# A recurrent transformer segment loop on one core: a weight ring kept across turns, and memory rows joined to the next tokens

## The chip, the core and the metric

The kernel runs on one core of one Trainium2 chip. TensorE (PE) multiplies, with its weight loads on a queue of their own (PEld); VectorE (DVE), ScalarE (ACT) and GpSimd (POOL) do the rest, and SyncE (SP) issues most of the transfers (DMAs). The metric is the time of one execution on the device, in microseconds (us); lower is better. Comparisons are between medians of runs on one chip.

## What is computed

Two independent halves stand side by side in the output. Half A is a dilated sliding attention over 2048 tokens (32 heads of 20, a window of 8). Half B is a transformer layer with a memory that goes through the sequence segment by segment:

```python
mem = mem0                                     # 8 x 640
for s in range(n_seg):                         # 64 segments of 32 tokens
    h = concatenate([mem, x[:, 32*s:32*s+32]])           # 40 rows of 640
    q, k, v = (einsum('btd,dhe->bhte', h, W) for W in (Wq, Wk, Wv))   # 32 heads of 192
    scores = where(mask, q k^T * scale, -1e9)  # mask: key is memory, or key <= query
    o = softmax(scores) v
    o = einsum('bhte,hed->btd', o, Wo)
    mem = o[:, :8];  outs.append(o[:, 8:])
```

The four weights are 640 x 6144 numbers each in bf16, 31.5 MB together, more than the core's SBUF holds. Each segment needs all of them, and a segment can't start before the memory rows of the one before are there.

## The kernel before, in words

The weights are cut into 64 units of 128 x 1920 numbers (480 KB), four heads at a time of one type: (Q, r, j), (K, r, j), (V, r, j) for r and j from 0 to 3, and 16 units (O, ..) of the output projection. 44 units stay in SBUF (`resident`, tiles w_..), 20 (`streamed`) are loaded in every turn from copies in DRAM (`ws_scr`, named ws_.._65 to ws_.._84 in the order in which a turn uses them, nearly every third unit) into a ring of five slots, the tile pool `b_ring`; its tiles show in the trace as t. `get(u)` (L359 to 364) issues the load at the place in the program where the unit is first used.

The work is staged. First come resident units, the copies of the streamed ones and half A (`run_a`). Then a phase L computes Q, K and V of the last 8 tokens of all segments at once, since they depend on no memory and nothing of the next segment depends on them in its own projections: x is loaded in 16 blocks of 128 rows and turned on TensorE (L253), the last 8 tokens of each segment go to XL, the first 24 to a scratch `xt_scr`, and the results to `qk_scr` and `v_scr`. The remaining 18 resident units are loaded behind L. Then four loops of 16 turns run `segment(s)`, one turn for each segment, and a tail projects the output of the last 8 rows.

In a turn HT holds the 32 rows (8 of memory, 24 of tokens) turned, 128 x 5 x 32. `proj` (L378) multiplies them by four units at a time, in 20 matmuls on four quarters of the array; `qk` brings Q and K out, `turn` turns them (L401, L404), `scores` and a softmax follow for each of two halves t, `vproj` makes V. `turn_p(t)` (L458) turns the probabilities P and those of the left-over rows, PL, a single tile that the softmax of either half writes (L439). `pv(t)` makes OT (L493), and `oproj` (L507) adds the output projection into Y, 12 matmuls for each unit. At the end DVE casts Y to ybf (L545), transposes it in 32 x 32 blocks into yt (L547) and copies the 8 memory rows into HT (L548); the 24 token rows of the next segment were put there by GpSimd (`put_x`, L346) from xt. ACT's queue stores ol_scr and, in four DMAs, the token rows of ybf (L550).

PE and SP run in the order in which the code is written (`manual_schedule`); a scheduler orders the other engines. So SP issues a turn's small loads between the weight loads: `load_left` (qkl, L337) behind `turn(2)`, whose GpSimd copies (L395) read the old qkl; `load_x` (xt, L343) behind `put_x`; `load_vl` (vl, L340) behind `pv(1)`, which reads the old vl. Each waits until the old content is read, and SP takes nothing else meanwhile. L364 is the line of the weight loads.

Of the kernel before, what the change touches and what calls it, by code (L numbers as in the profile page):

```python
# [149 lines left out]
def part_b(ctx, tc, B_x, B_mem0, B_Wq, B_Wk, B_Wv, B_Wo, out, ident, run_a):  # L150
# [8 lines left out]

    nc = tc.nc  # L160
# [6 lines left out]
    x2 = B_x.rearrange("b s d -> (b s) d")  # L167
# [39 lines left out]
    xt_scr = dram.tile([n_seg + 2, 128, 5 * NX], BF16, name="xt_scr")  # L207
# [21 lines left out]
    with ExitStack() as c1:  # L229
# [16 lines left out]

        XL = lone.tile([128, 5, n_seg, NL], BF16)
        for i in range(S // 128):
            xb = lx.tile([128, Dm], BF16, tag="xb")
            nc.sync.dma_start(xb[:], x2[128 * i:128 * i + 128, :])  # L250
            pt = lps.tile([128, 5, 4, SEG], BF16, tag="ps")
            for dc in range(5):
                nc.tensor.transpose(pt[:, dc].rearrange("p a b -> p (a b)"), xb[:, 128 * dc:128 * dc + 128], ident)  # L253
            xt = lx.tile([128, 4, 5, NX], BF16, tag="xt")
            cps[i % 2](xt[:].rearrange("p s c n -> p c s n"), pt[:, :, :, 0:NX])
            cps[(i + 1) % 2](XL[:, :, 4 * i:4 * i + 4, :], pt[:, :, :, NX:SEG])
            nc.sync.dma_start(xt_scr[4 * i:4 * i + 4].rearrange("s p n -> p s n"),
                              xt[:].rearrange("p s c n -> p s (c n)"))
        for k in range(2):
            nc.sync.dma_start(xt_scr[n_seg + k], xt[:, k].rearrange("p c n -> p (c n)"))  # L260
# [35 lines left out]
    ring = lctx.enter_context(tc.tile_pool(name="b_ring", bufs=N_RING))  # L296
# [11 lines left out]
    for g in range(2):  # L308
        m = mask[64 * g:64 * g + 64, :]
        nc.gpsimd.affine_select(out=m[:, NL:L], in_=m[:, NL:L], compare_op=ALU.is_ge, fill=-1e9, base=-NL,  # L310
                                pattern=[[-1, L - NL]], channel_multiplier=1)
        nc.gpsimd.memset(mask[64 * g:64 * g + NL + M, :], 0.0)
        nc.gpsimd.affine_select(out=m[:, 0:NL], in_=m[:, 0:NL], compare_op=ALU.is_ge, fill=-1e9, base=0,
                                pattern=[[-1, NL]], channel_multiplier=1)
        nc.gpsimd.affine_select(out=m[:, 0:NL], in_=m[:, 0:NL], compare_op=ALU.is_ge, fill=-1e9, base=NL + M - 1,
                                pattern=[[0, NL]], channel_multiplier=-1)
# [10 lines left out]

    QTW = 24 * L
    PL = cst.tile([128, 4, 4, NL], BF16)
    nc.gpsimd.memset(PL[:], 0.0)  # L330
# [3 lines left out]
    xt = cst.tile([128, 5, NX], BF16)  # L334
# [7 lines left out]
    def load_x(s):  # L342
        nc.sync.dma_start(xt[:].rearrange("p c n -> p (c n)"), xt_scr[s])  # L343

    def put_x():
        nc.gpsimd.tensor_copy(HT[:, :, M:32], xt[:])  # L346

    xr = one.tile([M, Dm], BF16, tag="xr")
    nc.sync.dma_start(xr[:], mem2)
    pm = acc([128, 5, M], BF16)  # L350
    for dc in range(5):
        nc.tensor.transpose(pm[:, dc, :], xr[:, 128 * dc:128 * dc + 128], ident[0:M, 0:M])
    nc.vector.tensor_copy(HT[:, :, 0:M], pm[:])
    load_x(0)
    put_x()
    load_left(0)
    load_vl(0)
    load_x(1)

    def get(u):  # L360
        if u in res:
            return view(res[u][:], u)
        t = ring.tile([128, US], BF16, tag="ws")
        nc.sync.dma_start(t[:], ws_scr[u][:])  # L364
        return view(t[:], u)

    def segment(s):
# [5 lines left out]
        def proj(ty, r):  # L373
            ps = acc([128, 384], name="pj")
            ws = [get((ty, r, j)) for j in range(4)]
            for dc in range(5):
                for j in range(4):
                    nc.tensor.matmul(ps[32 * j:32 * j + 32, :], lhsT=HT[:, dc, :], rhs=ws[j][:, dc, :],  # L378
                                     start=(dc == 0), stop=(dc == 4), tile_position=(0, 32 * j))
            return ps  # L380
# [7 lines left out]
        def turn(r):  # L388
            t = r // 2
            if r % 2 == 0:  # L390
# [3 lines left out]
                for T_, ty in ((QT, Q), (KT, K)):  # L394
                    nc.gpsimd.tensor_copy(T_[:, 0:QTW].rearrange("p (c j l) -> p c j l", c=6, j=4)[:, :, :, 0:NL],  # L395
# [6 lines left out]
            for T_, ty in ((cur["QT"], Q), (cur["KT"], K)):  # L402
                dst = T_[:, 0:QTW].rearrange("p (c j l) -> p c j l", c=6, j=4)[:, 3 * (r % 2):3 * (r % 2) + 3, :, NL:L]
                (nc.scalar.copy if ty == Q else nc.vector.tensor_copy)(dst, tp[:, ty])  # L404

        def scores(t):
# [13 lines left out]
            for n, (_, lo, rr, j, e, cc, hi) in enumerate(pl):  # L420
# [17 lines left out]
            nc.vector.tensor_tensor(P[t][:], t1[:, :, NL:L], sm[:].unsqueeze(2).to_broadcast([128, 8, 32]), op=ALU.mult)  # L438
            nc.vector.tensor_tensor(PL[:, :, 2 * t:2 * t + 2, :].rearrange("p j r k -> p r j k"),  # L439
                                    t1[:, :, 0:NL].rearrange("p (r j) k -> p r j k", r=2),  # L440
# [12 lines left out]
        def turn_p(t):  # L453
# [4 lines left out]
            nc.tensor.transpose(ptp[:, 2].rearrange("p e q -> p (e q)"), PL[:].rearrange("p j r k -> p (j r k)"), ident)  # L458
# [3 lines left out]
            nc.vector.tensor_tensor(PTL[:], ptp[:, 2, :, 0:16].unsqueeze(2).to_broadcast([128, 2, 2, 16]),  # L462
# [3 lines left out]
        def pv(t):  # L466
# [11 lines left out]
            for e in range(2):  # L478
                for j in range(4):
                    nc.tensor.matmul(ots[j][:, :, e, 0:16], lhsT=vl[G[j], e, 0:128], rhs=PTL[G[j], e], start=False,  # L480
# [187 lines left out]
```

## Time and profile before

| | us |
|---|---|
| median of 3 runs (5035.1 to 5046.54) | 5036.02 |
| the profiled execution | 4988.09 |
| its span, first to last instruction | 4986.3 |
| PE busy in the span | 2792.9 (56%) |
| PEld busy | 1755.1 (35%) |
| DVE, ACT, POOL busy | 1045.2, 605.4, 188.9 |

The page lists, for each group of instructions, the busy time, the mean time of one in ns, and the idle time of the engine just ahead of them with what ended it. A row on waits gives the engine, the line, what ended the waiting, the sum in us, how often and the longest. A row of the timeline gives the start and the length in us, the engine (SPq is SP's queue), line, operation and tiles, and in brackets the idle time ahead and its end. A row of windows gives the length of a stretch, each engine's busy time with its number of instructions, the granted TensorE clock as a share of its full 2.4 GHz, the mean busy share of the 16 DMA engines, and GB/s.

### The profile page before, as it was taken

What the parts mean: (1) busy time and instruction counts of PE and PEld (TensorE: products, weight loads), DVE (VectorE), ACT (ScalarE), POOL (GpSimd) and SP (SyncE); (2) the same over time, 40 slices, a digit from 0 to 9 for tenths busy, and PEclk for the clock granted to TensorE, in tenths of its full rate; (3) what the DMA queues carried; (4) which work ended last, traced back from release to release, by engine and by line L of the source; (5) the groups of instructions that cost most, each with busy time, mean ns of one, the idle gap of its engine ahead of it and who ended that gap; (6) DMA issues with size and microseconds to landing.
All of it is one profiled execution on the core that took longest, in us unless ns stands there. A gap on an engine that the chain in (4) does not pass through costs nothing. (4 is left out here: it accounts for less than half of the span.)

```text
span 4986.3 us, 107002 instructions
## 1 busy us (share of the span) xinstructions
PE 2792.9 (56%) x42572; PEld 1755.1 (35%) x42597; DVE 1045.2 (21%) x2433; ACT 605.4 (12%) x1444; POOL 188.9 (4%) x638
## 2 busy tenths in 40 slices
PE   1768555555555555555555555555555555555556
PEld 0543333333333333333333333333333333333334
DVE  1652111211112111111211111211111121121111
ACT  1222111111111111111111010111110111111111
POOL 0100000000000000000000000000000000000000
PEclk9988866666666666565666666566666566666667
DMA  8764844444444444444444444444444444444444
GB/s 242 247 214 118 254 159 152 157 165 153 152 149 151 158 154 157 161 143 151 143 152 162 160 143 153 143 155 156 157 165 140 157 146 155 155 157 165 150 155 143
DMA packets 388638, 803.95 MB, mean 161 GB/s; under 512 B 81768, under 2 KB 215600, under 8 KB 388576
## 3 DMA queue, kind: packets, MB, share of 16 engines
q1 hardware_dynamic: 325712, 756.93, 44.1%
q10 hardware_dynamic: 56880, 19.50, 1.6%
q0 software_dynamic: 5984, 26.67, 1.5%
q8 instruction: 42, 0.69, 0.1%
q14 instruction: 20, 0.16, 0.0%
HBM read 762.32 MB, written 50.47 MB: 163 GB/s over the span
## 5 line engine op out<-in xcount | busy, mean ns | idle before, releaser
L378 PE MATMUL pj<-t,HT 128*32 128x384 bf16 x4800 | 1193.3, 459 | 795.4 <-DMA t<-ws_3_2_74 298.0
L378 PEld LDWEIGHTS <-HT 128*32 128x32 bf16 x15360 | 546.8, 120 | 1524.9 <-issue 1192.7
L507 PEld LDWEIGHTS <-OT 128*32 128x32 bf16 x12288 | 482.5, 126 | 700.7 <-issue 593.2
L507 PE MATMUL Y<-t,OT 128*32 128x160 bf16 x3840 | 205.4, 323 | 599.1 <-DMA t<-ws_1_0_80 307.2
L385 ACT CAST nat<-pj 128x384 bf16<-128x384 f32 x256 | 121.5, 475 | 1709.4 <-PE pj L378 973.6
L385 DVE CAST nat<-pj 128x384 bf16<-128x384 f32 x256 | 142.8, 558 | 871.6 <-PE pj L378 810.6
L378 PE MATMUL pj<-w_0_0_147,HT 128*32 128x384 bf16 x320 | 120.1, 499 | 222.7 <-DVE HT L548 174.6
L458 PE MATMUL ptp<-ident,PL 128*128 128x128 bf16 x128 | 38.5, 301 | 293.4 <-DVE PL L439 293.4
L404 DVE COPY KT<-tp 128x384 bf16<-128x384 bf16 x256 | 91.1, 356 | 499.8 <-ACT QT L404 499.8
L404 ACT COPY QT<-tp 128x384 bf16<-128x384 bf16 x256 | 123.2, 481 | 481.1 <-PE L378 481.1
L493 DVE CAST OT<-ot 128x240 bf16<-128x240 f32 x256 | 92.5, 403 | 385.6 <-PE Y L507 240.2
L401 PE MATMUL tp<-ident,nat 128*128 128x128 bf16 x1536 | 167.2, 260 | 0.1
L401 PEld LDWEIGHTS <-nat 128*128 128x128 bf16 x1536 | 111.7, 115 | 115.7 <-issue 113.9
L545 DVE CAST ybf<-Y 128x160 bf16<-128x160 f32 x64 | 20.8, 325 | 612.9 <-remote 603.6
L422 PE MATMUL S<-KT,QT 128*64 128x40 bf16 (+1 forms) x4096 | 139.4, 190 | 8.6 <-DVE KT L404 7.6
L493 ACT CAST OT<-ot 128x240 bf16<-128x240 f32 x256 | 79.4, 362 | 531.1 <-PE pj L378 280.1
L462 DVE TENSOR_TENSOR PTL<-ptp,bd 128x64 bf16<-128x64 bf16 x128 | 24.5, 192 | 554.6 <-ACT PT L460 554.6
L422 PEld LDWEIGHTS <-QT 128*64 128x64 bf16 (+1 forms) x4096 | 117.2, 112 | 66.5 <-issue 59.8
L494 POOL COPY olt<-OT 128x192 bf16<-128x192 bf16 x128 | 44.4, 347 | 2168.1 <-ACT OT L493 1427.0
L458 PEld LDWEIGHTS <-PL 128*128 128x128 bf16 x128 | 16.3, 128 | 304.5 <-DVE PL L439 304.5
L378 PE MATMUL pj<-w_0_0_4235,HT 128*32 128x384 bf16 x320 | 123.4, 520 | 0.0
L378 PE MATMUL pj<-w_1_2_161,HT 128*32 128x384 bf16 x320 | 122.2, 505 | 0.0
(442 smaller groups left out, 5951.7 us busy)
## 6 DMA issues: line engine op xcount, KB each, us to landing
t<-ws_1_0_80 SPq DMA_DIRECT2D x66, 480.0 KB, 5.1
t<-ws_0_2_81 SPq DMA_DIRECT2D x66, 480.0 KB, 7.0
t<-ws_2_0_82 SPq DMA_DIRECT2D x66, 480.0 KB, 3.6
t<-ws_3_1_83 SPq DMA_DIRECT2D x66, 480.0 KB, 4.6
t<-ws_2_3_84 SPq DMA_DIRECT2D x66, 480.0 KB, 5.6
t<-ws_0_1_65 SPq DMA_DIRECT2D x65, 480.0 KB, 5.3
t<-ws_1_0_67 SPq DMA_DIRECT2D x65, 480.0 KB
t<-ws_1_3_68 SPq DMA_DIRECT2D x65, 480.0 KB, 7.2
```

The lines of the kernel that those rows point to most:

```text
L378: nc.tensor.matmul(ps[32 * j:32 * j + 32, :], lhsT=HT[:, dc, :], rhs=ws[j][:, dc, :], start=(dc == 0), stop=(dc == 4), tile_position=(0, 3 ...
L385: (nc.scalar.copy if ty == Q else nc.vector.tensor_copy)(n_[:], ps[:])
L401: nc.tensor.transpose(tp[:, ty, c].rearrange("p j l -> p (j l)"), n_[:, 128 * c:128 * c + 128], ident)
L404: (nc.scalar.copy if ty == Q else nc.vector.tensor_copy)(dst, tp[:, ty])
L422: nc.tensor.matmul(Sps[64 * e:64 * e + 64, 4 * rr + j, :], lhsT=QT[lo:hi, o:o + 64], rhs=KT[lo:hi, o:o + L], start=(e not in seen), stop=( ...
L458: nc.tensor.transpose(ptp[:, 2].rearrange("p e q -> p (e q)"), PL[:].rearrange("p j r k -> p (j r k)"), ident)
L462: nc.vector.tensor_tensor(PTL[:], ptp[:, 2, :, 0:16].unsqueeze(2).to_broadcast([128, 2, 2, 16]), bd[:, 2 * t:2 * t + 2].unsqueeze(1).to_br ...
L493: (nc.scalar.copy, nc.vector.tensor_copy)[j % 2](OTs[t][:, j], ots[j][:])
L494: nc.gpsimd.tensor_copy(olt[:, t], OTs[t][:].rearrange("p j r x l -> p (j r x) l")[:, :, 0:NL])
L507: nc.tensor.matmul(Yb[0][32 * g:32 * g + 32], lhsT=OTs[t][:, j, rr, x, NL:L], rhs=w[:, x, :].rearrange("p (c g q) -> p c g q", c=5, g=4)[: ...
L545: nc.vector.tensor_copy(ybf[:], Yb[0][:])
```

## The change

The ring becomes five tiles of their own that live through all turns. `done(us)`, called behind the last use of a unit, issues the load of the unit that stands five places further on in the cycle of 20, into the slot that has just been used; the first five loads stand ahead of the loops, and the last units of a turn are followed by the first loads of the next. PL becomes two tiles, one for each half. The rows of a segment are held as 24 tokens first and 8 memory rows last, and column blocks of 160 stand on the four quarters of the partitions; the rows of the weights are permuted to suit, so a Q, K or V unit is loaded by five DMAs, each from four blocks of 32 rows. The tokens of the next segment come as `xz`, untransposed with zeros in the memory rows (a scratch that DMAs fill straight from x), and one DVE instruction adds them to the memory rows of Y (`rows` is 1 there and 0 in token rows); one transpose then writes all of HT. ACT casts Y to yo for one store, and both stores go out on SP's queue. The L phase loads only the last 8 tokens, in four blocks. The core of the diff:

```diff
@@ weights
-    wv_ = [w.rearrange("(dc p) h e -> p dc (h e)", p=128) for w in (B_Wq, B_Wk, B_Wv)]
+    wv_ = [w.rearrange("(g c q) h e -> c g q (h e)", g=4, c=5) for w in (B_Wq, B_Wk, B_Wv)]
...
-            eng.dma_start(v, wv_[ty][:, :, 1536 * j + 384 * r:1536 * j + 384 * r + 384])
+            for c in range(5):
+                eng.dma_start(v[:, c, :], wv_[ty][c, :, :, 1536 * j + 384 * r:1536 * j + 384 * r + 384])
@@ the L phase
+        for g in range(4):
+            nc.scalar.dma_start(xz_scr[0:n_seg, g, 0:NX, :], x3[:, 0:NX, 160 * g:160 * g + 160])
...
-        for i in range(S // 128):
+        for i in range(NLT // 128):
             xb = lx.tile([128, Dm], BF16, tag="xb")
-            nc.sync.dma_start(xb[:], x2[128 * i:128 * i + 128, :])
...
+            nc.sync.dma_start(xb[:], x3[16 * i:16 * i + 16, NX:SEG, :])
@@ the ring
-    ring = lctx.enter_context(tc.tile_pool(name="b_ring", bufs=N_RING))
+    ws_ring = [cst.tile([128, US], BF16, name=f"ring{k}") for k in range(N_RING)]
+    def load_ring(k):
+        nc.sync.dma_start(ws_ring[k % N_RING][:], ws_scr[streamed[k % N_STR]][:])
...
     def get(u):
-        if u in res:
-            return view(res[u][:], u)
-        t = ring.tile([128, US], BF16, tag="ws")
-        nc.sync.dma_start(t[:], ws_scr[u][:])
-        return view(t[:], u)
+        return view(res[u][:] if u in res else ws_ring[pos[u] % N_RING][:], u)
+
+    def done(us):
+        for u in us:
+            if u in pos:
+                load_ring(pos[u] + N_RING)
@@ softmax, turn_p
-            nc.vector.tensor_tensor(PL[:, :, 2 * t:2 * t + 2, :].rearrange("p j r k -> p r j k"),
+            nc.vector.tensor_tensor(PLs[t][:, :, 2 * t:2 * t + 2, :].rearrange("p j r k -> p r j k"),
@@ the turn
         turn(2)
-        load_left(s + 1)
         qk(K, 3)
         vproj(0)
         turn(3)
         vproj(1)
+        load_left(s + 1)
...
         vproj(3)
-        put_x()
-        load_x(s + 2)
         oproj(0, 0, 4)
         turn_p(1)
         oproj(0, 4, 6)
         pv(1)
+        oproj(0, 6, 8)
+        oproj(1, 0, 4)
         load_vl(s + 1)
-        oproj(0, 6, 8)
-        nc.scalar.dma_start(ol_scr[s], olt[:].rearrange("p t x l -> p (t x l)"))
-        oproj(1, 0, 8)
-        ybf = one.tile([128, 5, 32], BF16, tag="ybf")
-        nc.vector.tensor_copy(ybf[:], Yb[0][:])
-        yt = one.tile([128, 5, 32], BF16, tag="yt")
-        nc.vector.transpose(yt[:].rearrange("p c q -> p (c q)"), ybf[:].rearrange("p c q -> p (c q)"))
-        nc.vector.tensor_copy(HT[:, :, 0:M], yt[:, :, 0:M])
-        for g in range(4):
-            nc.scalar.dma_start(out3[s][:, :, g, :], ybf[32 * g + M:32 * g + 32])
+        oproj(1, 4, 8)
+        nc.sync.dma_start(ol_scr[s], olt[:].rearrange("p t x l -> p (t x l)"))
+        z = one.tile([128, 160], BF16, tag="z", name="z")
+        nc.vector.scalar_tensor_tensor(out=z[:], in0=Yb[0][:], scalar=rows[:], in1=xz[:], op0=ALU.mult, op1=ALU.add)
+        nc.vector.transpose(HT[:].rearrange("p c t -> p (c t)"), z[:])
+        load_x(s + 2)
+        yo = one.tile([128, 160], BF16, tag="yo", name="yo")
+        nc.scalar.copy(yo[:], Yb[0][:])
+        nc.sync.dma_start(out3[s], yo[:])
```

The order of SP's queue from the first output-projection loads to the next turn, before (t is the ring's tile of the moment, ws_.. the copies in DRAM):

```order
L343 ISA
L343 DMA xt<-xt_scr 128x120
L364 ISA
L364 DMA t<-ws_1_0_80 128x1920
L364 ISA
L364 DMA t<-ws_0_2_81 128x1920
L340 ISA
L340 DMA vl<-v_scr 128x384
L364 REGISTER_ALU
L364 DMA t<-ws_2_0_82 128x1920
```

Here each small load stands right ahead of the weights that are used next. SP's queue at the end of a turn, after (ring_4485 to ring_4489 are the five slots):

```order
L355 ISA
L355 DMA ring_4488<-ws_1_3_68 128x1920
L349 ISA
L349 DMA vl<-v_scr 128x384
L355 ISA
L355 DMA ring_4489<-ws_1_2_69 128x1920
L553 ISA
L553 DMA ol_scr<-olt 128x384
L352 ISA
L352 DMA xz<-xz_scr 128x160
L561 ISA
L561 DMA out_dram<-yo 4x32x160
```

What moved: the weights around vl now belong to the next turn, and ol_scr, xz and the output store stand last, ahead of the next turn's first load, ws_2_1_70.

DVE at the end of a turn, before (Y is the output projection's sum, ybf and yt are its cast and its transpose):

```order
L545 REGISTER_ALU
L545 CAST ybf<-Y 128x160
L547 REGISTER_ALU
L547 STREAM_TRANSPOSE yt<-ybf 128x160
L548 REGISTER_ALU
L548 COPY HT<-yt 128x5x8
```

Cast, transpose and copy of the memory rows stand in a row. The same place after:

```order
L504 REGISTER_ALU
L504 CAST OT<-ot 128x240
L556 REGISTER_ALU
L556 SCALAR_TENSOR_TENSOR z<-Y,rows,xz 128x160
L557 REGISTER_ALU
L557 STREAM_TRANSPOSE HT<-z 128x160
```

Three instructions became two, and the transpose writes HT itself.

## Rows read from the trace of the kernel before

**Rows 1.** The page's costliest groups: the matmuls on ring tiles.

```profile
L378 PE MATMUL pj<-t,HT 128*32 128x384 bf16 x4800 | 1193.3, 459 | 795.4 <-DMA t<-ws_3_2_74 298.0
...
L507 PE MATMUL Y<-t,OT 128*32 128x160 bf16 x3840 | 205.4, 323 | 599.1 <-DMA t<-ws_1_0_80 307.2
```

**Rows 2.** Windows: start, prologue stretches, loop, and single microseconds at either clock.

```profile
0.00:50.00 50.00, 0.00 (x0) 0.00 (x0) 0.97 (x4) 1.28 (x1) 1.34 (x7) 1.00 1.00 286
...
610.00:4913.00 4303.00, 2369.83 (x39808) 1507.79 (x39808) 819.26 (x2112) 464.31 (x1152) 157.03 (x576) 0.62 0.44 154
...
2035.00:2036.00 1.00, 1.00 (x16) 0.47 (x12) 0.36 (x1) 0.46 (x1) 0.00 (x0) 0.50 0.96 277
2038.00:2039.00 1.00, 1.00 (x25) 0.45 (x22) 0.00 (x1) 0.86 (x2) 0.00 (x0) 1.00 0.12 46
...
360.00:390.00 30.00, 10.25 (x81) 6.85 (x81) 5.49 (x18) 6.82 (x16) 1.97 (x11) 0.58 0.66 145
390.00:600.00 210.00, 164.09 (x795) 79.36 (x804) 57.86 (x129) 50.41 (x128) 0.00 (x0) 0.90 0.57 174
```

**Rows 3.** Waits of TensorE for tiles other than ring tiles.

```profile
PE ptp L458 <- DVE PL L439: 293.4, 64, 4.8
...
PE pj L378 <- DVE HT L548: 174.6, 60, 5.1
...
PE pT L58 <- DMA xb<-in_A_x_dram: 89.2, 1, 89.2
```

**Rows 4.** Waits of SP's queue.

```profile
SPq L343 <- POOL HT L346: 1050.0, 64, 18.0
SPq L364 <- DMA out_dram<-ybf: 888.9, 240, 10.4
SPq L340 <- PE Y L507: 621.6, 64, 10.2
SPq L337 <- POOL KT L395: 478.7, 64, 8.6
```

**Rows 5.** The timeline of one turn, from 2020.90 to the next turn's start.

```profile
2021.43 0.32 SPq L364 DMA_DIRECT2D t<-ws_0_1_65  x1
...
2024.76 0.48 PE L378 MATMUL pj<-t,HT 128*32 128x384 bf16 x1 [3.38 <-DMA t<-ws_0_1_65]
...
2066.13 0.34 SPq L343 DMA_DIRECT2D xt<-xt_scr  x1
2066.68 0.32 SPq L364 DMA_DIRECT2D t<-ws_1_0_80  x1
...
2070.26 0.59 PE L507 MATMUL Y<-t,OT 128*32 128x160 bf16 x12 [4.92 <-DMA t<-ws_1_0_80]
...
2077.14 0.62 ACT L493 CAST OT<-ot 128x240 bf16<-128x240 f32 x2 [3.98 <-PE Y L507]
...
2077.64 0.36 SPq L364 DMA_DIRECT2D t<-ws_2_0_82  x1
...
2081.45 0.59 PE L507 MATMUL Y<-t,OT 128*32 128x160 bf16 x12 [4.43 <-DMA t<-ws_2_0_82]
...
2087.47 0.33 DVE L545 CAST ybf<-Y 128x160 bf16<-128x160 f32 x1 [9.61 <-remote]
...
2087.83 0.34 DVE L547 STREAM_TRANSPOSE yt<-ybf 128x160 bf16<-128x160 bf16 x1
2088.28 0.17 DVE L548 COPY HT<-yt 128x40 bf16<-128x40 bf16 x1
...
2088.71 0.48 PE L378 MATMUL pj<-w_0_0_147,HT 128*32 128x384 bf16 x1 [2.91 <-DVE HT L548]
```

**Rows 6.** The timeline: two successive steps of a projection, at either clock.

```profile
2035.36 0.53 PE L378 MATMUL pj<-w_1_0_163,HT 128*32 128x384 bf16 x1
...
2035.68 0.53 PE L378 MATMUL pj<-w_1_0_163,HT 128*32 128x384 bf16 x1
...
2038.07 0.34 PE L378 MATMUL pj<-t,HT 128*32 128x384 bf16 x1
...
2038.24 0.33 PE L378 MATMUL pj<-t,HT 128*32 128x384 bf16 x1
```

More of the change, by code (lines that the diff above doesn't have):

```diff
@@ L326, in part_b @@
     nc.vector.tensor_copy(bd[:], bdf[:].unsqueeze(2).to_broadcast([128, 4, 16]))
+    rows = cst.tile([128, 1], FP32)
+    nc.vector.tensor_copy(rows[:], bdf[:, 3:4])
     QTW = 24 * L
-    PL = cst.tile([128, 4, 4, NL], BF16)
-    nc.gpsimd.memset(PL[:], 0.0)
+    PLs = [cst.tile([128, 4, 4, NL], BF16, name=f"PL{t}") for t in range(2)]
+    for t in range(2):
+        nc.gpsimd.memset(PLs[t][:], 0.0)
     HT = cst.tile([128, 5, 32], BF16)
@@ L342, in load_x @@
     def load_x(s):
[L343 to L354, printed above, removed]
-    put_x()
+        nc.sync.dma_start(xz[:], xz_scr[s].rearrange("g t n -> (g t) n"))
+    def load_ring(k):
+        nc.sync.dma_start(ws_ring[k % N_RING][:], ws_scr[streamed[k % N_STR]][:])
+    z0 = one.tile([128, 160], BF16, tag="z")
+    nc.sync.dma_start(z0[:], xz_scr[0].rearrange("g t n -> (g t) n"))
+    for g in range(4):
+        nc.sync.dma_start(z0[32 * g + NX:32 * g + 32, :], mem2[:, 160 * g:160 * g + 160])
+    nc.vector.transpose(HT[:].rearrange("p c t -> p (c t)"), z0[:])
     load_left(0)
@@ L358, in part_b @@
     load_x(1)
+    for k in range(N_RING):
+        load_ring(k)
+    pos = {u: k for k, u in enumerate(streamed)}
     def get(u):
-        if u in res:
-            return view(res[u][:], u)
-        t = ring.tile([128, US], BF16, tag="ws")
-        nc.sync.dma_start(t[:], ws_scr[u][:])
-        return view(t[:], u)
+        return view(res[u][:] if u in res else ws_ring[pos[u] % N_RING][:], u)
[3 more added lines that the diff above has]
+                load_ring(pos[u] + N_RING)
     def segment(s):
@@ L379, in proj @@
                                      start=(dc == 0), stop=(dc == 4), tile_position=(0, 32 * j))
+            done([(ty, r, j) for j in range(4)])
             return ps
@@ L479, in pv @@
                 for j in range(4):
-                    nc.tensor.matmul(ots[j][:, :, e, 0:16], lhsT=vl[G[j], e, 0:128], rhs=PTL[G[j], e], start=False,
+                    nc.tensor.matmul(ots[j][:, :, e, NX:L], lhsT=vl[G[j], e, 0:128], rhs=PTL[G[j], e], start=False,
                                      stop=False, tile_position=(32 * j, 0), skip_group_check=True)
@@ L489, in pv @@
                 for j in range(4):
[L490 removed]
+                    nc.tensor.matmul(ots[j][64 * e:64 * e + 64, :, 2, NX:L], lhsT=vl[G[j], e, 128:192], rhs=PTL[G[j], e],
                                      start=False, stop=(e == 1), tile_position=(32 * j, 64 * e), skip_group_check=True)
@@ L506, in oproj @@
                     for g in range(4):
-                        nc.tensor.matmul(Yb[0][32 * g:32 * g + 32],
-                                         lhsT=OTs[t][:, j, rr, x, NL:L],
-                                         rhs=w[:, x, :].rearrange("p (c g q) -> p c g q", c=5, g=4)[:, :, g, :],
+                        nc.tensor.matmul(Yb[0][32 * g:32 * g + 32], lhsT=OTs[t][:, j, rr, x, 0:32],
+                                         rhs=w[:, x, 160 * g:160 * g + 160],
                                          start=(t == 0 and n == 0 and x == 0), stop=(t == 1 and n == 7 and x == 2),
                                          tile_position=(0, 32 * g))
+                done([(O, 2 * t + rr, j)])
         qk(Q, 0)
```

60 lines of the change are left out of this document (30 added, 30 removed).

## The prediction, made before the changed kernel had run

> **What bounds the kernel now.** I began with the costliest groups of the page and with what ended the idle time before each. TensorE has the most busy time, yet two of its rows have more idle time behind them than anything else in the loop: the matmuls on weights out of the ring (named t) waited 795.4 us in the projections and 599.1 us in the output projection, each time for a DMA [rows 1]. That is 1394.5 us, or 21.8 us of each of the 64 turns. The loop takes 4303 us, 67.2 us a turn, and in it the DMA engines are busy 0.44 of the time [rows 2], so it isn't the amount that is loaded that sets the time, but when the loads start.
>
> The waits of TensorE's other inputs come next: 293.4 us for PL, 4.6 us a turn, and 174.6 us for HT, 2.7 us a turn [rows 3]. Then I asked SP, which issues the loads in a fixed order, what it waits for: 1050.0 us for GpSimd's copy into HT ahead of the xt load, 888.9 us for landings of the out stores ahead of weight loads, 621.6 us for TensorE ahead of the vl load, 478.7 us for GpSimd's KT ahead of the qkl load [rows 4]. None of these is a wait for a free slot. A small load that must wait stands in the queue, and the weight loads behind it stand too.
>
> One turn shows it. Weight 80 is issued at 2066.68, right behind the xt load of 2066.13, and TensorE gets it at 2070.26 after 4.92 us of idleness; 82 is issued at 2077.64 and awaited until 2081.45, 4.43 us; at the turn's start 65 is issued at 2021.43 and awaited until 2024.76, 3.38 us [rows 5]. So a lone load takes 3.3 to 3.8 us from issue to matmul, and TensorE pays nearly all of it, since each is issued when TensorE is about to need it.
>
> Last I asked what is left of a turn when nothing waits. The loop has 39808 matmuls and as many weight loads on TensorE [rows 2], 1244 instructions a turn. From 2070.26 to the cast of OT at 2077.14, which needs the last of them, TensorE does five weight units of the output projection (24 instructions each), 6 for one turn of P and 96 for pv, 222 in all, in 6.88 us: 31.0 ns each. From 2081.45 to the ybf cast at 2087.47 it does eight units, 192, in 6.02 us: 31.4 ns [rows 5]. Neither stretch has a wait, both hold other shapes, and the pace is the same. I take 31 ns as the least that an instruction costs here over a long stretch, whatever its size: 1244 x 31 ns = 38.6 us. Projections are slower than that at the low clock: their steps come every 0.32 us there (five steps, 1.6 us for 40 instructions) and every 0.17 us at the high one [rows 6], at granted clocks of 0.50 and 1.00 [rows 2], that is 1.2 and 2.4 GHz. At 31 ns the 40 cost 1.24 us, so a projection at the low clock costs 0.36 us more, twelve of them 4.3 us.
>
> **The change part by part.** *The ring.* A load goes out when the unit five places ahead has been used, across turns too. Twelve projections use 15 of the 20 streamed units, so the lead of five units is four projections, at least 4 x 1.24 = 5.0 us of TensorE, against 3.3 to 3.8 us for a load; in the output projection a unit comes every 24 x 31 ns = 0.74 us and every third or fourth is streamed, so the lead is some 12 us. The 21.8 us go. What this costs: the 20 loads, 9.8 MB, must fit in the turn. At the loop's 154 GB/s over a share of 0.44 [rows 2], full engines would move 350 GB/s, so 9.8 MB and some 0.5 MB of small ones need 29 us of a turn. Busy share 0.69 of 42.6 us; it fits, unevenly.
>
> *SP's order.* The qkl load moves behind vproj(1), four steps later than turn(2), where its last reader is queued; vl behind four units of the last output half; xz to the end. The waits of [rows 4] that were for GpSimd or for DVE-fed work no longer stand before a weight that is needed soon. What is new on SP is the end of the turn: ol_scr, xz and out stand there, and out waits for ACT's copy of Y, which exists only when all of the turn's matmuls are done. Queued behind it is load 70, for the slot that unit 65 leaves, used in qk(Q,2). Moreover the program hands its DMAs eight completion semaphores in turn, and by that count 70 has that of the out store, so it waits for its landing, as SP does now for out stores [rows 4], 888.9 us over 240 waits, 3.7 us each. The store goes out about 1 us behind the last cast and lands some 3 us later; 70 wants to be issued about 1.5 us into the turn and used 5 us later. Bounds 0 and 2 us a turn; I take 0.8.
>
> *PL in two tiles.* turn_p(0) no longer reads what softmax(1) writes. The 4.6 us of PL go; the second half's stands before turn_p(1), behind vproj(2), pv(0), vproj(3) and four units, over 5 us of TensorE. Cost nothing, and if that cover failed, at most the old 4.6.
>
> *The turn's end.* Cast 0.33, transpose 0.34, copy 0.17 on DVE and the gaps take from 2087.47 to 2088.71, 1.24 us [rows 5]. The scalar_tensor_tensor that replaces the cast reads the same 128x160 from the same place; the trace has no row of it: between the cast's 0.33 and twice that; I take 0.33, since the size and the source are the same. The copy goes with its gap, about 0.28. So 1.0 us remains, 1.3 at the upper bound. ACT's copy yo is off this path; the new 40 KB store takes the place of four.
>
> Sum of a turn: 38.6 + 2.2 (half of the twelve projections at the low clock; all would be 4.3, none 0) + 1.0 + 0.8 = **42.6 us**. From above: 67.2 - 21.8 - 4.6 = 40.8, less 0.28, plus 0.8 = 41.3. I keep the first, as waits that now let a backlog drain will be gone. Loop: 64 x (67.2 - 42.6) = -1574 us.
>
> *The prologue.* Its weight loads take another form: five DMAs per unit, and each names on the source side four blocks of 32 rows where it named 128 rows. 66 units of 0.49 MB are so loaded: 30 ahead of part A's first x, 18 within the L phase, 18 ahead of the loop. In the first 50 us all 16 engines are busy at a share of 1.00 and move 286 GB/s [rows 2], 17.9 each. No row shows how a transfer of four blocks is dealt out. If over all 16, nothing changes. If by block over four, they move 71.5 GB/s together, a unit takes 6.9 us instead of 1.7, and the 32.4 MB take 453 us instead of 113. If on one engine, 1812 us. I take four: it is the only count that the new form has and the old hadn't. The Trainium skill states it so: "DMA: Bandwidth & Descriptors", section "Why a DMA increments its semaphore by 16 and not by 1", has a transfer use the largest number up to 16 that divides the first dimension of both sides, always the lowest-numbered engines; by that rule it is four, the same four each time, and no run here shows it. On four engines the 30 units take 206 us instead of 52, and part A waits for its x behind them, now 89.2 us [rows 3]: +155. L has 210 us [rows 2], and its 18 units (124 us instead of 31) lie largely beside its matmuls: +10, at most +93. The 18 ahead of the loop stand alone: +93 at most; the first turn uses them one after another, so I take +85. The 16 blocks that build XL, 30 us [rows 2], become four: -23. Sum **+227 us**, between -23 (16 engines) and +318.
>
> Against the profiled execution: 4988.1 - 1574 + 227 = 3641. The median of the runs stands 1.0096 above the profiled time (5036.02 over 4988.09), which gives 3676; I say **3675**.
>
> **The rivals.** (1) *The weights still go over 16 engines.* For it: they do so now; against it: the four blocks. 4988.1 - 1574 - 23 = 3391, times 1.0096: 3424.
>
> (2) *The ring becomes the bound.* In the projections the lead is four projections, and if loads that are queued behind one another take longer than that, each late slot delays the next. For it: at 2035 the DMA engines are at a share of 0.96 while TensorE works [rows 2]. Against it: over a turn 29 us of 42.6. Twelve stalls of 0.4 us, or a 4.5 us stall behind load 70: turn 47.1, loop -1286, 4988.1 - 1286 + 227 = 3929, times 1.0096: 3967.
>
> (3) *The clock stays high.* If no projection falls to 1.2 GHz and 70 isn't late, the turn is 38.6 + 1.0 = 39.6: -1766, 3449, times 1.0096: 3482. The loop's granted clock is now 0.62 [rows 2] with 27 us of waiting a turn, most of which goes. The Trainium skill says so of it ("TensorE: Matmul & The Clock Gate", "Part 1: The HAM clock gate"): the clock follows how busy the array has been. Against it: from 2035 TensorE is busy throughout, and the clock is 0.50 [rows 2]. Here the trace speaks for half and half.
>
> (4) *Slower: the weights go on a single engine.* If the new form puts each transfer on one engine, 32.4 MB at 17.9 GB/s are 1812 us, 1699 more than now; it decides from the point where the prologue grows by more than the loop gives back, 1574. 4988.1 - 1574 + 1699 - 23 = 5090, times 1.0096: 5139. Against it: the source has four blocks, and both sides would have to be dealt out by less than that.
>
> (5) *The change doesn't do what it says.* If SP is held at the out store as long as it now is held at xt and vl, the loads stay late and only PL and the copy are gained, 4.9 us a turn: 4988.1 - 314 + 227 = 4901, times 1.0096: 4948. Against it: only one of 20 loads stands directly behind that store with the slot free.
>
> **How the numbers follow.** Chances: forecast 0.62, (1) 0.12, (2) 0.13, (3) 0.08, (4) 0.02, (5) 0.03. The forecast's own range is turns of 41 to 45 us with a prologue of +150 to +318, 3500 to 3910. The range reaches down over (1) and (3) and leaves out (2), (4) and (5), 0.18: 3410 to 3930. A measurement of this kernel tells differences of about 0.3% from none; all cases but (4) are faster by more than that, with a little left for a tie: faster 0.97, same 0.01, slower 0.02.
>
> **What would show it.** Right: TensorE's rows on ring tiles lose their DMA waits; no wait for PL; the wait for HT stays at 2 to 3 us a turn; SP waits for TensorE alone, and for the out store at most once a turn; a turn is 41 to 45 us, the loop's DMA share 0.65 to 0.75; the first 50 us show 70 to 100 GB/s at a share near 0.3, and part A waits for x 200 to 250 us. Wrong: 286 GB/s at the start (rival 1); DMA waits on ring tiles in the Q and K projections (rival 2); a granted clock over 0.9 (rival 3). A turn under 38.6 us would fell the 31 ns.

## The result and the profile after

The median fell from 5035.56 to **3523.33 us** (four runs each, 3521.12 to 3534.18 after); the ratio is 0.700, with a 95% interval of 0.698 to 0.702. The prediction said 3675, with a range of 3410 to 3930. The profiled execution took 3534.18 us with a span of 3532.4.

Windows of the changed kernel: its first 50 us, and its loop, from the first projection to the last output projection.

```profile
0.00:50.00 50.00, 0.00 (x0) 0.00 (x0) 0.97 (x4) 0.00 (x0) 1.34 (x7) 1.00 0.65 152
...
833.50:3455.00 2621.50, 2125.61 (x39808) 1584.13 (x39808) 779.49 (x2046) 483.32 (x1215) 138.59 (x512) 0.88 0.75 252
```

The loop answers to the row of 4303 us in [rows 2]: 2621.5 us, 41.0 us a turn in place of 67.2, with the same number of TensorE instructions, at a granted clock of 0.88 where it was 0.62. (The row of 4303 us runs some 6 us past the last output projection; to the same point as here it was 67.1.) But the loop starts at 833.5 us and not at 610: the prologue grew by 223 us. The first 50 us move 152 GB/s at a share of 0.65, not the 70 to 100 at 0.3 that the prediction named as a sign; from 60 to 200 us it is 110 at 0.35. The first resident units are of the output projection, whose loads kept their form.

The page's costliest groups: two of the five ring slots.

```profile
L388 PE MATMUL pj<-ring_4488,HT 128*32 128x384 bf16 x960 | 223.4, 371 | 51.7 <-DMA ring_4488<-ws_3_3_73 43.9
...
L388 PE MATMUL pj<-ring_4485,HT 128*32 128x384 bf16 x960 | 206.4, 349 | 48.5 <-DMA ring_4485<-ws_2_1_70 43.9
```

They answer to [rows 1]: the ring tiles of the projections once had 795.4 us of idleness ahead of them; now the two worst slots have 100 and all five 144. In the output projection 599.1 us became 31.0, and these are for OT, not for a load (the row on Y below). What is left is late landings of 73 and, as foreseen, of 70, the load that stands behind the output store: 0.7 us a turn each. TensorE's waits in the loop and the first waits of SP:

```profile
PE pj L388 <- DVE HT L557: 156.5, 60, 2.6
...
PE ot L486 <- ACT PT L471: 68.1, 115, 0.7
...
PE Y L518 <- ACT OT L504: 31.0, 64, 0.5
...
SPq L355 <- PE L518: 782.1, 251, 5.6
SPq L355 <- PE pj L388: 287.7, 259, 7.0
```

No wait for PL is among them, HT's is 2.4 us a turn, and SP's largest waits are now for TensorE to be done with a slot; none of its rows names GpSimd [rows 4]. The turn's end, in the timeline:

```profile
2063.22 0.38 DVE L556 SCALAR_TENSOR_TENSOR z<-Y,rows,xz 128x160 bf16<-128x160 f32 x1 [6.60 <-issue]
...
2063.64 0.35 DVE L557 STREAM_TRANSPOSE HT<-z 128x160 bf16<-128x160 bf16 x1
...
2064.08 0.32 PE L388 MATMUL pj<-w_0_0_147,HT 128*32 128x384 bf16 x1 [2.61 <-DVE HT L557]
```

From the first DVE instruction to TensorE it takes 0.86 us, where it took 1.24 [rows 5].

### The profile page after: what moved, and what is told of

It reads as the page before. It is cut to its first block, busy times and chain, and to the rows that moved or that the text cites. A ratio compares the mean times of both kernels' runs of the same rounds, so it can differ in the third digit from the quotient of the medians.

```text
span 3532.4 us, 106126 instructions
## 1 busy us (share of the span) xinstructions
PE 2561.1 (73%) x42567; PEld 1831.5 (52%) x42592; DVE 1002.5 (28%) x2357; ACT 618.7 (18%) x1494; POOL 170.1 (5%) x572
## 5 line engine op out<-in xcount | busy, mean ns | idle before, releaser
L388 PEld LDWEIGHTS <-HT 128*32 128x32 bf16 x15360 | 479.4, 104 | 701.4 <-issue 204.5
L518 PEld LDWEIGHTS <-OT 128*32 128x32 bf16 x12288 | 614.3, 102 | 113.1 <-ACT OT L504 102.9
L388 PE MATMUL pj<-w_0_0_147,HT 128*32 128x384 bf16 x320 | 75.3, 373 | 278.4 <-DVE HT L557 156.5
L388 PE MATMUL pj<-ring_4488,HT 128*32 128x384 bf16 x960 | 223.4, 371 | 51.7 <-DMA ring_4488<-ws_3_3_73 43.9
L388 PE MATMUL pj<-ring_4487,HT 128*32 128x384 bf16 x960 | 236.8, 371 | 22.4 <-PE S L433 13.7
L388 PE MATMUL pj<-ring_4485,HT 128*32 128x384 bf16 x960 | 206.4, 349 | 48.5 <-DMA ring_4485<-ws_2_1_70 43.9
L388 PE MATMUL pj<-ring_4489,HT 128*32 128x384 bf16 x960 | 240.4, 381 | 0.2 <-DMA ring_4489<-ws_3_2_74 0.2
L388 PE MATMUL pj<-ring_4486,HT 128*32 128x384 bf16 x960 | 220.2, 367 | 21.0 <-DMA ring_4486<-ws_2_0_71 16.6
L412 PE MATMUL tp<-ident,nat 128*128 128x128 bf16 x1536 | 154.8, 234 | 27.5 <-DVE nat L396 26.9
L412 PEld LDWEIGHTS <-nat 128*128 128x128 bf16 x1536 | 95.0, 103 | 134.3 <-issue 90.3
L58 PE MATMUL pT<-ident,xb 128*128 128x128 bf16 x80 | 8.3, 241 | 215.5 <-DMA xb<-in_A_x_dram 212.5
L556 DVE SCALAR_TENSOR_TENSOR z<-Y,rows,xz 128x160 bf16<-128x160 f32 x64 | 24.6, 384 | 422.1 <-issue 422.1
L496 PE MATMUL ot<-PT,Vn 32*64 32x40 bf16 x2048 | 123.6, 182 | 0.0
L486 PE MATMUL ot<-PT,Vn 32*128 32x40 bf16 x2048 | 71.8, 178 | 68.5 <-ACT PT L471 68.1
```

What stands on the lines that cost most here:

```text
L58: nc.tensor.transpose(pT[:, c, :], xb[:, c * 128:(c + 1) * 128], ident)
L412: nc.tensor.transpose(tp[:, ty, c].rearrange("p j l -> p (j l)"), n_[:, 128 * c:128 * c + 128], ident)
L486: nc.tensor.matmul(ots[j][:, rr, e, :], lhsT=Vn[G[j], 2 * t + rr, e, 0:128], rhs=PT[G[j], rr, e, :], start=(rr == 0 and e == 0), stop=Fals ...
L496: nc.tensor.matmul(ots[j][64 * e:64 * e + 64, rr, 2, :], lhsT=Vn[G[j], 2 * t + rr, e, 128:192], rhs=PT[G[j], rr, e, :], start=False, stop= ...
L518: nc.tensor.matmul(Yb[0][32 * g:32 * g + 32], lhsT=OTs[t][:, j, rr, x, 0:32], rhs=w[:, x, 160 * g:160 * g + 160], start=(t == 0 and n == 0 ...
L556: nc.vector.scalar_tensor_tensor(out=z[:], in0=Yb[0][:], scalar=rows[:], in1=xz[:], op0=ALU.mult, op1=ALU.add)
```

## The experiments

GpSimd's copies inside a turn are written as a multiplication by one in all kernels of this section; c0 is the changed kernel with that alone and is what the others are held against (e5, made from the kernel before, has the same form). Every ratio is to the kernel before on the same chip; c0 and e1 to e3 ran on one chip, where that took 5035.01 us, e4 to e11 on another, where it took 5029.73 and 5031.72.

```diff
-                nc.gpsimd.memset(QT[:, QTW:QTW + 24], 0.0)
+                nc.gpsimd.tensor_tensor(QT[:, QTW:QTW + 24], z24[:], z24[:], op=ALU.mult)
...
-                    nc.gpsimd.tensor_copy(T_[:, 0:QTW].rearrange("p (c j l) -> p c j l", c=6, j=4)[:, :, :, 32:L],
-                                          qkl[:, ty, 6 * t:6 * t + 6])
+                    nc.gpsimd.tensor_tensor(T_[:, 0:QTW].rearrange("p (c j l) -> p c j l", c=6, j=4)[:, :, :, 32:L],
+                                            qkl[:, ty, 6 * t:6 * t + 6], o1[:].unsqueeze(2).unsqueeze(3).to_broadcast([128, 6, 4, NL]), op=ALU.mult)
```

> The changed kernel with GpSimd's copies inside a turn written as a multiplication by one (GpSimd is off the path that sets the turn: its longest wait for work is 15 us). Every other run is compared with this one. Expected: within 0.5% of the changed kernel, 3510 to 3545 us. If GpSimd's KT copy holds the scores, some 64 x 0.3 us more.

3523.55 us, ratio to before 0.699 (0.698 to 0.701), 40.97 us a turn: no difference. GpSimd's form doesn't matter here.

### The loop: ring, SP's order, PL

e2 undoes the ring:

```diff
-        return view(res[u][:] if u in res else ws_ring[pos[u] % N_RING][:], u)
+        if u in res:
+            return view(res[u][:], u)
+        t = ring.tile([128, US], BF16, tag="ws")
+        nc.sync.dma_start(t[:], ws_scr[u][:])
+        return view(t[:], u)
     def done(us):
-        for u in us:
-            if u in pos:
-                load_ring(pos[u] + N_RING)
+        pass
```

> The changed kernel with the ring as it was (a pool of five, each load at the place of use, nothing loaded ahead across turns); SP's order, PL and the turn's end stay changed. Theory (ring and SP's order share the gain; what only the ring can give is the turn's start): the first four loads of a turn are issued after the output store, and TensorE waits again some 3.4 + 0.6 + 1.1 + 1.7 = 6.8 us a turn, turn 47 to 48.5, about 3960 us. Rival (SP's order alone did it): under 1 us a turn more, below 3590 us. Rival (the ring alone did it): most of the 21.8 us a turn come back, above 4600 us.

4050.91 us (ratio 0.804, 0.802 to 0.806): 527 us more, 49.2 us a turn, some 90 us above the first theory and far from either rival. e4 takes back SP's order instead:

```diff
         turn(2)
+        load_left(s + 1)
...
         vproj(1)
-        load_left(s + 1)
...
         pv(1)
+        load_vl(s + 1)
         oproj(0, 6, 8)
         oproj(1, 0, 4)
-        load_vl(s + 1)
```

> The changed kernel with the qkl load back behind turn(2) and the vl load back behind pv(1); ring, PL, turn's end and the place of xz stay changed. Theory (a small load that waits holds the weight loads behind it, and the ring's lead covers only a part): SP stands at qkl and at vl for some us each, 2 to 6 us a turn, 3650 to 3900 us. Rival (with the ring kept SP's order doesn't matter): below 3550 us.

3523.59 us (ratio 0.700, 0.698 to 0.702): no difference, as the rival had it. And e5 gives the kernel before the ring and nothing else, with the old order, one PL, the old turn's end and the old weight loads:

```diff
+    ws_ring = [cst.tile([128, US], BF16, name=f"ring{k}") for k in range(N_RING)]
+    for k in range(N_RING):
+        load_ring(k)
...
-        t = ring.tile([128, US], BF16, tag="ws")
-        nc.sync.dma_start(t[:], ws_scr[u][:])
+        return view(res[u][:] if u in res else ws_ring[pos[u] % N_RING][:], u)
...
+            done([(ty, r, j) for j in range(4)])
...
+                done([(O, 2 * t + rr, j)])
```

> The kernel before with the ring alone: five tiles kept across turns, each load behind the last use of the unit five places ahead; the small loads, PL, the turn's end and the weights' form stay as before. Theory (ring and order are about additive; undoing the ring cost 8.4 us a turn): 8 to 11 us a turn gained, 4330 to 4530 us. Rival (the lead of five units covers what SP's small loads hold up): nearly all of the 21.8 us gained, below 3900 us. Rival (without the order the ring gives nothing): above 4900 us.

3888.03 us (ratio 0.773, 0.771 to 0.776), 49.8 us a turn. TensorE's largest wait in e2, where the ring's tiles are named t:

```profile
PE pj L389 <- DMA t<-ws: 503.8, 273, 10.3
```

In e4, its wait for ring tiles, and what SP waits for at the vl load:

```profile
PE pj L392 <- DMA ring<-ws: 113.3, 158, 4.5
...
SPq L353 <- PE Y L523: 203.9, 64, 3.2
```

In e5, three of TensorE's waits:

```profile
PE ptp L471 <- DVE PL L452: 294.8, 64, 4.6
PE tp L414 <- ACT nat L398: 276.7, 60, 6.8
...
PE pj L390 <- DMA ring<-ws: 24.5, 48, 2.6
```

With the ring alone the waits for ring tiles all but vanish, from 1394.5 us in [rows 1] to 24.5 in the largest row left. SP still stands, 3.2 us a turn at vl in e4, and in e5 436.8 us in all for landings of out stores ahead of weight loads, but these loads are for units five places on, and the lead covers it. So the ring is enough without the order, and with the ring the old places of qkl and vl cost nothing; my reading that a held queue is what makes TensorE wait was true only as long as each load was issued at its place of use.

The ring isn't the only way to most of the gain, though. e2, without it, waits 7.9 us a turn for weights and not 21.8, and its turn of 49.2 us is even shorter than e5's 49.8 (PL and the casts' wait are gone from it too). So what else changed takes some 14 of the 21.8 us by itself: SP's order, the stores' move, xz in place of xt or several of these, which were not tried apart without the ring. The two remedies overlap; only the ring takes nearly all of these waits away.

e5 shows a cost that the profile of before had hidden. ACT's queue in e5, at the start of a turn:

```profile
2012.56 7.58 ACTq L565 DMA_DIRECT2D out_dram<-ybf  x4
2020.78 0.86 ACT L398 CAST nat<-pj 128x384 bf16<-128x384 f32 x2 [15.28 <-DMA out_dram<-ybf]
```

To issue four stores of 64-byte runs keeps ACT's queue for 7.58 us, and the first two casts of Q wait behind them; TensorE waits 276.7 us, 4.3 a turn, for those casts. In the kernel before the stores took as long, but were covered, as TensorE stood some 5 us a turn at the loads 65, 66 and 67 (222.2, 45.9 and 63.7 us in all). A row of its timeline and one of its waits:

```profile
2020.02 7.20 ACTq L550 DMA_DIRECT2D out_dram<-ybf  x4
...
PE pj L378 <- DMA t<-ws_0_1_65: 222.2, 64, 13.1
```

The move of the store to SP, as one DMA of 320-byte runs, which I had priced at nothing, should therefore be worth up to 4.3 us a turn once the ring is there; no run moved the store alone.

e3 puts the two PL tiles back into one, in the softmax and in turn_p:

```diff
-    PLs = [cst.tile([128, 4, 4, NL], BF16, name=f"PL{t}") for t in range(2)]
+    PL = cst.tile([128, 4, 4, NL], BF16)
```

> The changed kernel with one PL tile for both halves. Theory: the wait of 4.6 us a turn comes back but for what TensorE has still to hand on when it begins, so 3 to 4.6 us a turn, 3720 to 3820 us. Rival (PL was only waiting beside another wait): no change, below 3550 us.

3795.84 us (ratio 0.754, 0.752 to 0.755): 272 us more, 4.25 a turn. TensorE's row of waits for PL is back:

```profile
PE ptp L472 <- DVE PL L453: 301.4, 64, 4.9
```

Together: 67.1 us a turn before, less 17.3 for the ring alone (49.8 in e5), less 4.2 for PL (e3 against c0), less 4.3 read from e5's row for the casts, gives 41.3; measured 41.0, the turn's end having lost 0.4. The parts aren't quite additive: c0 also waits 1.5 us a turn more for ring tiles than e5.

### How near the ring is to its limit

e9 takes one slot away:

```diff
-    N_STR, N_RING, N_LOOPS = 20, 5, 4
+    N_STR, N_RING, N_LOOPS = 20, 4, 4
```

> The changed kernel with a ring of four slots, each load one unit later. Theory (the ring is near its limit in the projections): the waits on ring tiles, now some 1.9 us a turn, rise by 1 to 4 us, 3590 to 3780 us. Rival (the lead is ample): below 3545 us.

3695.48 us (ratio 0.734, 0.732 to 0.736), 43.6 us a turn, 2.6 more; TensorE's waits for ring tiles rise from 121.6 us in c0:

```profile
PE pj L392 <- DMA ring<-ws: 304.2, 380, 4.8
```

One slot fewer costs more than qkl and vl in their old places. e8 takes the output store out, behind which load 70 stands:

```diff
         nc.scalar.copy(yo[:], Yb[0][:])
-        nc.sync.dma_start(out3[s], yo[:])
```

> The changed kernel without the store of the token rows in the turns (the output's token rows of half B are left out; ACT's copy yo stays). Theory (load 70 waits for the landing of that store, since both have one completion semaphore): TensorE's wait for 70, 43.9 us in all, and some of the waits of 71 and 73 behind it go, 45 to 80 us, 3445 to 3480 us. Rival (TensorE has instructions to hand on meanwhile, the wait is only moved): 3510 to 3530 us.

3520.41 us (3507.77 to 3536.25; ratio 0.701, 0.698 to 0.703): no difference that can be told. TensorE's waits for ring tiles do fall, in e8 to 86.3 us:

```profile
PE pj L392 <- DMA ring<-ws: 86.3, 110, 2.4
```

A third of them go and the time stays within the runs' own spread. The wait on the store is there: behind the turn's last transpose, load 70 goes out 3.6 us later on average in c0 and 2.3 us later in e8. The stall of 0.8 us that I charged is in the trace too, but removing it gives back 0.4 us a turn in the profiled loop (40.6 against 41.0), in the fastest of e8's four runs, and e1, which leaves the loop alone, has 40.6 as well. So nothing certain comes back in the time.

### What bounds a turn now

e6 leaves out instructions, e7 leaves out columns:

```diff
 e6, oproj
-                for x in range(3):
+                for x in range(2):
 e7, proj
+                    n_ = 384 if dc in (0, 4) else 96
-                    nc.tensor.matmul(ps[32 * j:32 * j + 32, :], lhsT=HT[:, dc, :], rhs=ws[j][:, dc, :],
+                    nc.tensor.matmul(ps[32 * j:32 * j + 32, 0:n_], lhsT=HT[:, dc, :], rhs=ws[j][:, dc, 0:n_],
```

> The changed kernel with the last third of each unit left out of the turn's output projection (two of three row blocks): 64 matmuls and 64 weight loads fewer a turn, so the output is not the layer's. Theory (a turn costs 30 to 31 ns for each of TensorE's instructions): 128 x 30 ns = 3.8 us a turn less, 3270 to 3290 us. Rival (columns set the time; 64 x 160 columns on four quarters at 2.4 GHz are 1.1 us): 3440 to 3470 us.

> The changed kernel with three of the five matmul steps of each projection cut to 96 of their 384 columns; the number of instructions is the same, the output is not the layer's. Theory (30 to 31 ns an instruction, whatever its size): within 0.5 us a turn, 3490 to 3530 us. Rival (columns set the time: 144 matmuls a turn lose 288 columns each, on four quarters at 2.4 GHz 4.3 us): about 3250 us.

e7: 3533.69 us (ratio 0.702, 0.701 to 0.704), no gain from 45% fewer columns in the projections. e6: 3380.47 us (0.672, 0.670 to 0.674), 143 us less. Windows on whole loops, first c0's:

```profile
825.80:3447.70 2621.90, 2113.93 (x39808) 1579.61 (x39808) 780.37 (x2046) 484.24 (x1215) 214.90 (x512) 0.89 0.75 252
```

The loop of e7:

```profile
829.00:3455.20 2626.20, 2029.66 (x39808) 1590.19 (x39808) 787.83 (x2046) 482.41 (x1215) 214.74 (x512) 0.78 0.75 252
```

The loop of e6:

```profile
831.60:3293.60 2462.00, 1865.27 (x35712) 1296.72 (x35712) 779.63 (x2046) 485.16 (x1215) 214.79 (x512) 0.81 0.79 268
```

e7 has the same instructions as c0, less work in them and a lower granted clock, 0.78 against 0.89, and takes the same 41.0 us a turn. So neither columns nor the clock set much of the time; the number of instructions does. e6 has 128 fewer a turn and gains 2.5 us, less than 128 x 30 ns = 3.8. The missing part is waits that grew as TensorE came sooner, in e6:

```profile
PE ot L490 <- ACT PT L475: 100.6, 118, 1.1
...
PE Y L523 <- ACT OT L508: 61.4, 64, 1.0
```

against 68.1 and 31.0 us in the changed kernel, and 158.7 in place of 121.6 for the ring: 100 us, 1.6 a turn, and 2.5 + 1.6 is 4.1, somewhat more than the 3.8.

The semaphore events of TensorE's instructions, one for each matmul and each weight load, which the trace also has, say it more directly. In the changed kernel's loop 98.7% of them follow the one before by 30 ns (95.3% in the kernel before), and none by less than 29. A turn of c0 is then 1244 x 30 ns = 37.3 us and 3.7 us in which the events pause. In e6 the pauses are 5.0 us, 1.3 more, and 3.8 - 1.3 is the 2.5 that were gained.

The events also show what the low clock costs. In c0's loop 396 of them lie 110 ns behind the one before, 378 of these at a granted clock of 0.50; that is 80 ns more than 30 each, 0.5 us a turn. e7 has one such event. Its waits grew meanwhile, for ring tiles from 121.6 us and for nat from 36.3, together by 1.2 us a turn, and its pauses come to 3.7 us again:

```profile
PE pj L393 <- DMA ring<-ws: 152.5, 147, 5.1
...
PE tp L417 <- DVE nat L401: 85.1, 111, 1.4
```

So the columns might be worth some 0.5 to 1.2 us a turn if those waits were not there, not the rival's 4.3; e7 as it stands shows nothing gained. Every one of these instructions raises a semaphore; whether the 30 ns belong to the instruction or to raising the semaphore, no run tried.

### The prologue

e1 loads each unit by four DMAs over 32 rows with all five blocks in place of five over 4 x 32 rows, and e10 makes it one:

```diff
 e1
-    wv_ = [w.rearrange("(g c q) h e -> c g q (h e)", g=4, c=5) for w in (B_Wq, B_Wk, B_Wv)]
+    wv_ = [w.rearrange("(g c q) h e -> g q c (h e)", g=4, c=5) for w in (B_Wq, B_Wk, B_Wv)]
...
-            for c in range(5):
-                eng.dma_start(v[:, c, :], wv_[ty][c, :, :, 1536 * j + 384 * r:1536 * j + 384 * r + 384])
+            for g in range(4):
+                eng.dma_start(v[32 * g:32 * g + 32], wv_[ty][g, :, :, 1536 * j + 384 * r:1536 * j + 384 * r + 384])
 e10
-    wv_ = [w.rearrange("(g c q) h e -> c g q (h e)", g=4, c=5) for w in (B_Wq, B_Wk, B_Wv)]
+    wv_ = [w.rearrange("(p c) h e -> p c (h e)", c=5) for w in (B_Wq, B_Wk, B_Wv)]
+            eng.dma_start(v, wv_[ty][:, :, 1536 * j + 384 * r:1536 * j + 384 * r + 384])
...
-                                         rhs=w[:, x, 160 * g:160 * g + 160],
+                                         rhs=w[:, x, 160 * g:160 * g + 160].rearrange("p (q c) -> p c q", c=5),
```

> Each Q, K and V unit loaded by four DMAs of 32 rows x 5 x 384 in place of five of 4 x 32 rows x 384; the bytes land in the same places. Theory (a transfer from four blocks runs on 4 of 16 engines): the loads run on all engines again, the start of the loop goes from 833 us back to some 585 us (610 less the 25 us saved at XL), the loop stays: 3275 to 3300 us. Rival (the number of DMAs costs, 330 in place of 66): 264 DMAs remain, so the loop's start stays above 780 us, about 3490 us.

> The changed kernel with the rows of the model permuted otherwise: partition p holds rows 5p to 5p+4 of a weight, so a Q, K or V unit is one DMA over 128 partitions again; the output projection, the sum with xz and yo read or write with a stride of five numbers. Theory (of the 223 us by which the loop starts later, four engines cost 151, and the number of DMAs, 330 in place of 66, the other 97, with 25 saved at XL): the loop starts at 580 to 590 us, 3255 to 3285 us. Rival (the V part of phase L is longer for another reason): the loop starts above 620 us, 3300 us and more. If strided reads cost TensorE or VectorE time in the loop, the turn grows beyond 41 us.

e1: 3357.05 us (ratio 0.666, 0.665 to 0.668), the loop starts at 682 us. e10: 3293.5 us (0.654, 0.653 to 0.656), the loop starts at 607 us and takes 40.7 us a turn. Both theories were right in part: the starts came 97 and some 20 us later than they said. Windows on the V part of phase L and the loads ahead of the loop, in the changed kernel:

```profile
620.00:739.00 119.00, 72.42 (x322) 34.33 (x320) 17.99 (x38) 14.98 (x33) 1.51 (x9) 0.80 0.57 173
739.00:833.00 94.00, 0.00 (x0) 0.00 (x0) 0.53 (x2) 0.23 (x1) 0.00 (x0) 0.51 0.30 99
```

The same two stretches of e1:

```profile
525.00:645.00 120.00, 68.16 (x319) 34.82 (x317) 18.53 (x39) 15.50 (x33) 1.49 (x9) 0.77 0.64 181
645.00:682.00 37.00, 0.00 (x0) 0.00 (x0) 0.50 (x1) 0.00 (x0) 0.00 (x0) 0.54 1.08 254
```

Where loads run alone, the changed kernel keeps 0.30 of the engines busy at 99 GB/s, and e1 all of them at 254: the form with four blocks uses about a quarter of the engines (0.27 at 93 GB/s from 770 to 810 us, within that stretch). That is the count in the rule of the Trainium skill ("DMA: Bandwidth & Descriptors", "Why a DMA increments its semaphore by 16 and not by 1") that the prediction cited, and here the runs agree with it; which four engines they are, the trace doesn't show. The wait for part A's first x goes from 212.5 to 118.4 us and the last loads from 94 to 37: together the 151 us by which e1 starts its loop sooner. The V part stays at 120 us in e1 and is 78 in e10 (505.3 to 583.6), as before the change: there it isn't the engines but, it seems, the four or five DMAs that take the place of one in SP's queue, between the stores of V. SP's rows fit that: it is busy issuing for 94.4 of the 119 us here, 94.1 of 120 in e1 and 66.5 of 78 in e10. e10 also gives each DMA 128 partitions where e1 gives it 32, which no run took apart.

### A version that beats both

e11 takes e10 and spends fewer instructions on the output projection.

```diff
-                for x in range(3):
-                    for g in range(4):
-                        nc.tensor.matmul(Yb[0][32 * g:32 * g + 32], ..., rhs=w[:, x, 160 * g:160 * g + 160], ...)
+                for h in range(2):
+                    for x in range(3):
+                        m = (8 * t + n) * 3 + x
+                        g = m % 4
+                        nc.tensor.matmul(Yb[h][32 * g:32 * g + 32], ..., rhs=w[:, x, 320 * h:320 * h + 320],
+                                         start=m < 4, stop=m >= 44, tile_position=(0, 32 * g), ...)
...
+        for c in range(5):
+            nc.tensor.matmul(hp[:, c, :], lhsT=ys[:].rearrange("k (p c) -> k c p", c=5)[:, c, :], rhs=selm[:], ...)
+        nc.vector.tensor_copy(HT[:], hp[:])
```

> The kernel of e10 with an output projection of fewer instructions and nothing left out: its 48 row blocks go in turn to the four column groups of the array, two matmuls of 320 columns each, and the four partial sums are added by five matmuls that also turn the rows, into which five others put the next tokens: 168 of 1244 instructions fewer a turn. Theory (30 ns an instruction): 5.0 us less, some 0.7 us more for the longer chain at the turn's end, 4.3 us a turn or 275 us less than e10, 2980 to 3010 us. Rival (320 columns a matmul bound it at the low clock): 2 us a turn, about 3140 us.

**3080.66 us** (ratio to before 0.612, 0.610 to 0.615), 213 us below e10, with 37.5 us a turn; the window on its loop:

```profile
601.50:3003.60 2402.10, 1884.54 (x34432) 1199.15 (x34432) 786.77 (x2048) 540.03 (x1343) 215.49 (x512) 0.86 0.80 276
```

168 instructions fewer (2 x 5376 over 64 turns) gave 3.25 us, between the two theories. Of TensorE's waits the largest that grew against e10 are the ring's, 165.4 in place of 120.2 us, and OT's, 74.8 in place of 26.5, and the new chain at the turn's end adds one of 82.4 for ACT's half of ys:

```profile
PE pj L394 <- DMA ring<-ws: 165.4, 144, 4.6
...
PE hp L570 <- ACT ys L568: 82.4, 64, 1.9
PE Y L527 <- ACT OT L510: 74.8, 64, 1.2
```

In the terms of the semaphore events, 168 x 30 ns are 5.0 us, and the pauses grew from 3.4 to 5.2 us a turn. So the theory's 30 ns held (97.7% of the events of e11's loop lie that far apart), and what it had too small was the waits, 1.8 us where it gave the longer chain 0.7; how the chain, the ring and the 320 columns share them was not tried apart, and it is not shown which part of the pauses each wait makes.

## Why the prediction was right, and where it wasn't

- **The waits go (right).** The term of 21.8 us a turn for ring waits held: 1.9 are left. That they were the bound was read from the right rows.
- **Why they go (wrong in part).** I put the waits down to SP's queue and gave the order its share. e5 shows that the ring alone takes them away, and e4 that the places of qkl and vl, with it, are worth nothing; e2 shows that without the ring the rest of the change takes 14 of the 21.8 us.
- **PL (right).** 4.6 us forecast, 4.25 measured in e3, where the page had 4.6.
- **The ACT stores (missed).** The new store was priced at nothing, and what the four old ones hold up was not seen; e5 shows 4.3 us a turn that would have come to light once the ring waits were gone. The change happens to move them away, so by luck the sum didn't suffer.
- **The least that a turn costs (right, and the pivot).** 1244 instructions at 31 ns were the base of the sum. e6 and e7 show that number, far more than columns or clock, sets it; the pace is nearer to 30, 37.3 us.
- **Projections at the low clock and the waits left over (mis-sized).** 2.2 us were added for half of the projections at 1.2 GHz. The loop's granted clock is 0.88, so about a quarter of the time is at the low level, and the events that come late there cost 0.5 us a turn in c0. Half of the projections was too many: 21% of their matmuls start at a granted clock of 0.50. At the 0.36 us that I charged for a projection this would still be 0.9 us. On the other side 41.0 less 37.3 leaves 3.7 us of pauses, those 0.5 and 3.2 of waits, for HT, OT, PT and ring tiles, where the sum had 2.2 and 1.0 + 0.8. So 42.6 - 1.3 (base) - 1.7 (low clock) + 1.4 (waits) = 41.0, and 102 us over the loop; the errors cancel in part. The sum from above, 41.3, which I set aside, came nearer. Rival (3), 39.6 us with the clock high throughout, lay about as far off on the other side. The Trainium skill's statement on the clock ("TensorE: Matmul & The Clock Gate", "Part 1: The HAM clock gate"), that it follows how busy the array has been, agrees: with the waits gone the granted clock rose from 0.62 to 0.88.
- **Load 70 (right in the rows, not in the time).** 0.7 us a turn are there; e8 could not find them in the time.
- **The prologue (right sum by luck, wrong parts).** +227 forecast, +223 measured. The parts: x of part A +123 (forecast +155), L +42 (+10), the loads ahead of the loop +75 (+85), XL -25 (-23), part A itself +8 (0). The step that failed is that L's loads lie beside its matmuls: in the V part they don't, 119 us for 78. e1 and e10 point to the number of DMAs, which the prediction had not priced. The 32 us that L cost too much and the 32 that the first x came sooner than forecast hide each other.
- **The step from profile to median.** I scaled by 1.0096, as before; after, the profiled execution lies 0.3% above the median. That is 46 of the 152 us between forecast and result; the loop is the other 102, and 4 are the prologue's.

## What to carry to other kernels

When a wait of 20 us in a turn goes, look for what it was covering: here ACT's store issues came next. Here a load's lead in units of work was worth more than its place in a queue; count how many units ahead it is issued, and only then argue about order. And look at a DMA's first dimension on both sides before changing a layout: a form that is neat for the inner loop made the prologue's loads run on a quarter of the engines.

## What the chip showed that I had not expected

TensorE's completions follow one another at 30 ns, for matmuls of 384, 160 and 96 columns and for weight loads alike: 45% fewer columns in the projections and a clock of 0.78 in place of 0.89 changed the turn by less than 0.1 us, while leaving out instructions paid at once. And a matmul operand read with a stride of five numbers (e10) cost nothing that shows: 40.7 us a turn against 41.0.
